# Attention and gated FFN on one core: paired attention bursts, a new order of the first loads, and DMA transposes from unit 7 on

## The chip, the cores and the metric

The kernel runs on one core of a Trainium2 chip. The metric is the device time of one execution in microseconds (us), as the median of several runs. A profile of one execution stands beside it. In it, PE is the matmul engine (TensorE), PEld its weight loads, DVE is VectorE, ACT is ScalarE, POOL is GpSimd, and SP is the engine that issues most of the DMAs.

## The reference, cut to what matters

Attention with a sliding window of 128 and four sink keys, followed by a gated feed-forward layer (FFN), with batch 4, 8 heads, 768 positions, head size 64, and 512 to 1536 to 512 in the FFN:

```python
scores = scale * np.matmul(q, k.transpose(0, 1, 3, 2))
keep = is_sink | in_window            # pos < 4, or 0 <= query - key < 128
a = softmax(np.where(keep, scores, -1e9))
x = (a @ v) with heads side by side   # 3072 x 512
gate = np.maximum(x @ w_gate, 0.0)
val = x @ w_val
out = gate * val @ w_out
```

All arrays are float32 in memory; the kernel computes in bfloat16 with float32 sums.

## The kernel before, in words

**Units.** Attention is cut into 16 units, `U[0]` to `U[15]`: unit i is batch i // 4 and a pair of two heads. For one unit the steps are:

- *Load*: `load_kq("k")`, `load_kq("q")` and `load_v` (three DMAs) bring float32 data into one of four staging tiles `stg`. A unit's five DMAs are issued one after another. `held(x)` (line 328) puts a tiny DVE memset ahead, so that the loads can't start before DVE has got there.
- *Cast*: `casts` turns K, Q and V into bfloat16 (`kn`, `qn`, `vn`), on POOL unless another engine is named.
- *Transpose*: K and Q must have the head dimension on the partitions (`kT`, `qT`). A unit whose flag `xbar` (line 95) is false does it on PE: `T` (line 140), twelve transposes into PSUM and two copies by ACT. A unit whose flag is true does it by two DMAs that SP issues: `X` (line 134). The flag also changes the layout of the K and Q loads: without it each partition reads two runs of 1536 bytes, with it twelve runs of 256 bytes.
- `sinkk` (line 155): two DVE copies from `kT` to `kTs`, which puts the sink keys beside the window keys. They wait for `kT`.
- `S(0)`, `S(1)`, `S(2)` (line 167): scores of a group of key blocks (64x128 matmuls, two heads at once), exp on ACT, and the mask multiply on DVE. In batch 0 the mask is instead added by a bias matmul.
- `norm(u, part)` (line 253), for two halves: `V` (line 187) makes the sums and the weighted values by 128x64 matmuls, and four DVE operations divide and write `xT`.

**Chunks.** The FFN is cut into 96 chunks (`chunk`, line 270), 24 for each batch: one of two halves of 384 positions by one of twelve blocks of 128 hidden columns. A chunk is four matmuls into `gp`, relu on ACT, four matmuls into `vp`, and the DVE multiply into `hT`. `gp` and `vp` take turns in three PSUM buffers (`ps_gv`); S and V of a unit take turns in two (`ps_at`) once the chunks have begun. The second FFN matmul, `ffn2` (line 287), goes three at a time behind each chunk as soon as half a batch is complete; it multiplies with `wo`.

**Order.** The order on every engine is that of the program; nothing reorders it. A list `stages` holds the attention work: a first stage and then six for each unit, made by `unit_stages` (line 360): `s(0)`, `v`, `s(1)`, `t`, `s(2)` and the `norm` of part 0. `v` is the `norm` of part 1 of the unit before. `s(0)` also issues `X` of the next unit. `t` prepares the next unit (`T` or nothing, then `sinkk`), issues one unit's loads and a part of the weights, and casts the unit three further on. `PLAN` (line 414) says how many stages have to be out before chunk ci: the pairs (ci, number of stages) are joined by straight lines, so that one stage falls to about every chunk. When chunk 24 begins, batch 1 is being multiplied while batch 2's attention is on its way.

**Weights.** POOL's queue loads `w_gate` and `w_val` in four column parts (`load_w`), and `w_out` in three row parts (`load_wo`); these loads stand in the order of POOL's casts. `load_wo(0)`, `(1)` and `(2)` are issued in stage `t` of units 5, 6 and 7, ahead of that stage's casts.

**Start.** K of unit 0 is loaded by SP and Q of unit 0 by ACT; V of unit 0 and all other loads follow on SP. POOL builds the identity and the first two bias patterns (`setup_pool`), DVE the rest (`setup_m0`, `setup_m1`). Sixteen matmuls on the identity warm PE.

Of the kernel before, what the change touches and what calls it, by code (L numbers as in the profile page):

```python
# [33 lines left out]
def kernel(  # L34
# [12 lines left out]
    nc = tc.nc  # L47
    B, H, S, D = q.shape
    assert (B, H, S, D) == (4, 8, 768, 64)
    NP = H // 2  # L50
# [21 lines left out]
    kT = [const.tile([128, 872], BF16, name=f"kT{i}") for i in range(2)]  # L72
# [15 lines left out]
    class Unit:  # L88
# [3 lines left out]
        def __init__(self, i):  # L92
            self.i, self.b, self.p, self.s = i, i // NP, i % NP, i % 2
            self.kn, self.qn, self.vn, self.stg = kn[i % 3], qn[i % 3], vn[i % 4], stg[i % 4]
            self.xbar = self.b>1
            self.biased = self.b == 0

        def staging(self, x):
# [24 lines left out]

        def cast(self, what, eng):

            if what in "kq":
                eng.tensor_copy((self.kn if what == "k" else self.qn)[:],  # L127
                                self.staging(what).rearrange("p h (n d) -> p n h d", d=64))
                return
            eng.tensor_copy(self.vn[:, 0:6, :, :], self.staging("v")[:, 0:6, :, :])  # L130
            eng.tensor_copy(self.vn[0:24, 6, :, :], self.staging("v")[0:24, 6, :, :])  # L131
            eng.tensor_copy(self.vn[0:4, 1:6:2, :, :], bc(self.vn[0:4, 0, :, :], 3))  # L132
# [7 lines left out]
        def T(self, first):  # L140

            s = self.s
            if first:
                ps = ps_gv.tile([128, 1024], BF16, name="tk", tag="gv")[:]
                pq = ps_op.tile([128, 1024], BF16, name="tq", tag="op")[:]
            else:
                both = ps_at.tile([128, 2, 1024], BF16, name="tkq", tag="at")
                ps, pq = both[:, 0, :], both[:, 1, :]
            for x, p_ in ((self.kn, ps), (self.qn, pq)):
                for t in range(6):  # L150
                    nc.tensor.transpose(p_[:, t * 128:(t + 1) * 128], x[:, t, :, :].rearrange("p h d -> p (h d)"), ident[:])
            for p_, dst, cp in ((ps, kT[s], nc.scalar.copy), (pq, qT[s], nc.scalar.copy)):
                cp(dst[:, 0:S].rearrange("d (p n) -> d p n", n=6), p_[:, 0:S].rearrange("d (n p) -> d p n", n=6))

        def sinkk(self):

# [50 lines left out]
    def load_w(c):  # L207
        n = d_ff // 4
        for w, dst in ((moe_w_gate, wg), (moe_w_val, wv)):
            nc.gpsimd.dma_start(out=dst[:, :, c * n:(c + 1) * n],  # L210
                                in_=w.rearrange("(ko ki) n -> ki ko n", ki=128)[:, :, c * n:(c + 1) * n])
# [16 lines left out]
    def setup_slot(s):  # L228
        nc.vector.memset(kT[s][:, S:872], 0.0)

    cp, ms = nc.vector.tensor_copy, nc.vector.memset

    def setup_m0():

        ms(bias[0:4, 0:128], 0.0)
        ms(bias[0:4, 128:255], NEG)
        cp(bias[:, 255:503], bias[:, 503:751])
        ms(bias[0:4, 255:503], 0.0)
        ms(bias[0:4, 503:627], NEG)

    def setup_m1():

        band, sk = (lambda a, b: bias[:, 503 + a:503 + b]), (lambda n: bias[:, 255:255 + n])
        cp(bias[:, 754:1002], sk(248))
        cp(bias[:, 1002:1253], band(0, 251))
        cp(bias[:, 1253:1397], sk(144))
        cp(bias[:, 1397:1417], band(0, 20))
        nc.vector.tensor_scalar(out=msk[:], in0=bias[:], scalar1=-1.0, scalar2=None, op0=Alu.is_ge)
# [53 lines left out]
    with tc.manual_schedule():  # L302
        U = [Unit(i) for i in range(B * NP)]
        on_array = []

        def at(x):
            return U[x] if 0 <= x < len(U) else None

        def casts(u, what, eng=nc.gpsimd):
            for w in what:  # L310
                u.cast(w, eng)

        warm_ps = []

        def warm(n):

            if not warm_ps:
                warm_ps.append(ps_at.tile([128, 2, 512], F32, name="warm", tag="at"))
            for _ in range(n):
                nc.tensor.matmul(out=warm_ps[0][:, 0, 0:128], lhsT=ident[:], rhs=ident[:], start=True, stop=True,  # L320
                                 skip_group_check=True)

        def load(x):
            U[x].load_kq("k", nc.sync)
            U[x].load_kq("q", nc.sync)
            U[x].load_v(nc.sync)

        def held(x):

            if x < len(U):  # L330
                nc.vector.memset(U[x].stg[0:1, 0:1], 0.0)
                load(x)

        U[0].load_kq("k", nc.sync)
        U[0].load_kq("q", nc.scalar)
        U[0].load_v(nc.sync)
        for x in range(1, 4):
            load(x)
        nc.vector.memset(ones[:], 1.0)
        setup_pool()  # L340
        nc.scalar.activation(ee[0][:, 0, 0, 0:64], ones[:], Act.Exp, bias=0.0, scale=1.0)
        for x in range(4):
            nc.vector.memset(vn[x][:, 6, :, :], 0.0)
        setup_slot(0)
        setup_slot(1)
        setup_m0()

        warm(16)
        casts(U[0], "k")
        casts(U[0], "q", nc.vector)  # L350
        casts(U[0], "v")
        casts(U[1], "kqv")
        casts(U[2], "kqv")
        load(4)
        setup_m1()


        stages = []

        def unit_stages(x):  # L360
            u, prev, nxt = U[x], at(x - 1), at(x + 1)

            def s(gi):
                def f():
                    if gi == 0 and u.p == 0:
                        xTs[u.b] = xpool.tile([128, NP, S], BF16, name="xT")
                    if gi == 0 and nxt is not None and nxt.xbar:
                        nxt.X()
                    u.S(gi)
                return f  # L370

            def v():
                if prev is not None:
                    norm(prev, 1, ps_at if on_array else ps_gv)

            def t():
                if nxt is not None:
                    if not nxt.xbar:
                        nxt.T(not on_array)
                    nxt.sinkk()  # L380
                if x == 0:
                    load_w(0)
                    load(5)
                elif x == 1:
                    load_w(1)
                elif x == 3:
                    load_w(2)
                    load(6)
                elif x == 4:
                    load_w(3)  # L390
                    load(7)
                elif 5 <= x:
                    held(x + 3)
                    if x < 8:
                        load_wo(x - 5)
                if at(x + 3) is not None:
                    casts(at(x + 3), "kqv")
            return [s(0), v, s(1), t, s(2), lambda: norm(u, 0, ps_at if on_array else ps_gv)]

        def first():  # L400
            U[0].T(True)
            U[0].sinkk()
        stages.append(first)
        for x in range(len(U)):
            stages += unit_stages(x)
        stages.append(lambda: norm(U[-1], 1))

        si = 0
        f2 = deque()
        total = len(stages)  # L410

        ORDER = [(0, h, m) for g in range(0, FM, 3) for h in range(2) for m in range(g, g + 3)]
        ORDER += [(b, h, m) for b in range(1, B) for h in range(2) for m in range(FM)]
        PLAN = ((0, 28), (24, 50), (48, 74), (71, 98))

        def want(ci):
            for (c0, w0), (c1, w1) in zip(PLAN, PLAN[1:]):
                if ci <= c1:
                    return w0 + (w1 - w0) * (ci - c0) // (c1 - c0)
            return total  # L420
        count = {}
        n = S // 2
        for ci, (b, h, m) in enumerate(ORDER):
            if b not in hTs:
                hTs[b] = hpool.tile([128, FM, S], BF16, name="hT", tag="hT")
            while si < min(total, want(ci)):
                stages[si]()
                si += 1
            if not ci:
                on_array.append(1)  # L430
            chunk(b, h * n, n, m)
            for _ in range(min(3, len(f2))):
                f2.popleft()()
            count[b, h] = count.get((b, h), 0) + 1
            if count[b, h] == FM:
                for t in range(3 * h, 3 * h + 3):
                    for mm in range(FM):
                        f2.append(lambda b=b, t=t, mm=mm: ffn2(b, t, mm, tail=b == B - 1))
        while f2:
            f2.popleft()()  # L440
# [33 lines left out]
```

The softmax here doesn't subtract the row's maximum and nothing guards it: scores larger than these inputs give would overflow.

## Time and profile before

| | |
|---|---|
| median of 8 runs | 265.59 us (263.9 to 269.19) |
| the profiled execution, whole | 265.92 us |
| its span, first to last instruction | 264.1 us |
| mean granted PE clock | 0.994 |
| DMA packets | 77318, of them 64496 under 512 bytes |
| wait of DVE for ACT's kT, in all | 7.0 us, 5 times |
| wait of POOL's kn cast for the K loads, in all | 33.7 us, 6 times |

The span is the time between the first and the last instruction of the profiled execution; 1.8 us lie around it. A row of the timeline gives the start, the length, the engine, the line of the code, the operation with the tiles written and read, and how many instructions were merged into the row. In brackets stand the idle time of the engine before it and what ended that. The row of a group of matmuls begins with the first and lasts to the modelled end of the last, so that successive rows overlap. "SPq" is the queue of SP: its rows show how long an issue kept it.

### The profile page before, as it was taken

Reading aid. Unit: us, or ns where it says so; the run is one execution under the profiler, and the core shown is the slowest. Engines: PE = TensorE matmul, PEld = TensorE weight load, DVE = VectorE, ACT = ScalarE, POOL = GpSimd, SP = SyncE. Lnnn points to the kernel's source line nnn. Section 1 sums busy time; section 2 is a strip of 40 time slices with the busy share of each in tenths; the row PEclk is TensorE's granted clock in tenths of the full one; section 3 lists DMA queues with packets and bytes.
Section 4 is the critical chain, followed back from the end, with each engine's and each line's share of the span. In section 5 each row is a group of like instructions: output and inputs, shape, how many; then the busy total and the mean of one; then the engine's idle time right before and its main releaser. Section 6 shows DMA issues by size and latency. Waiting matters only on the chain.

```text
span 264.1 us, 5117 instructions
## 1 busy us (share of the span) xinstructions
PE 250.6 (95%) x1968; PEld 139.4 (53%) x1992; DVE 145.6 (55%) x318; ACT 115.4 (44%) x186; POOL 63.0 (24%) x102
## 2 busy tenths in 40 slices
PE   3999899999978999999999999999999999999994
PEld 3555555665544555555555555555555555555441
DVE  3399969777762566665747566575656232322100
ACT  2777855656423444344344434434433323333211
POOL 5787359524213040221305050000000000000000
PEclk9999999999997999999999999999999999999999
DMA  7999999997989390939469391311011011111132
GB/s 195 313 293 222 245 242 230 222 228 138 177 134 199 93 220 10 236 86 174 109 139 181 83 201 40 63 40 42 0 42 40 2 41 40 40 42 40 40 119 79
DMA packets 77318, 33.54 MB, mean 127 GB/s; under 512 B 64496, under 2 KB 74224, under 8 KB 77296
## 3 DMA queue, kind: packets, MB, share of 16 engines
q1 hardware_dynamic: 71216, 28.12, 47.7%
q0 software_dynamic: 5808, 4.72, 11.4%
q10 hardware_dynamic: 272, 0.39, 0.4%
q8 instruction: 15, 0.25, 0.4%
q14 instruction: 7, 0.06, 0.1%
HBM read 28.51 MB, written 6.29 MB: 132 GB/s over the span
## 4 chain that ended last, share of the span: by engine, by line
PE 69%; DMA 18%; SPq 5%; POOL 3%; issue 3%; ACT 0%; POOLq 0%; ACTq 0%
PE op L294 23%; PE gp L275 20%; PE vp L281 18%; DMA stg<-in_v_dram 11%; PE ops L201 5%; DMA stg<-in_q_dram 5%; PE sps L179 3%; SPq L120 3%; DMA wo<-in_moe_w_out_dram 3%; SPq L112 2%; POOL vn L132 1%; SPq L122 1%; POOL vn L131 1%; POOL vn L130 1%; POOL qn L127 0%
## 5 line engine op out<-in xcount | busy, mean ns | idle before, releaser
L275 PE MATMUL gp<-xT,wg 128*128 128x384 bf16 x384 | 79.3, 330 | 0.0
L281 PE MATMUL vp<-xT,wv 128*128 128x384 bf16 x384 | 78.6, 328 | 0.5 <-DVE R L260 0.4
L278 ACT ACTIVATE gs<-gp 128x384 f32<-128x384 f32 x96 | 47.1, 490 | 72.8 <-PE gp L275 72.1
L283 DVE TENSOR_TENSOR hT<-gs,vp 128x384 bf16<-128x384 f32 x96 | 52.8, 551 | 43.1 <-PE vp L281 40.9
L294 PE MATMUL op<-wo,hT 128*128 128x512 bf16 x264 | 70.9, 380 | 3.8 <-DMA wo<-in_moe_w_out_dram 2.5
L183 ACT ACTIVATE ee<-sps 128x1006 bf16<-128x1006 f32 (+2 forms) x48 | 46.2, 965 | 39.1 <-PE sps L179 39.1
L281 PEld LDWEIGHTS <-wv 128*128 128x128 bf16 x384 | 37.8, 98 | 26.1 <-issue 1.6
L275 PEld LDWEIGHTS <-wg 128*128 128x128 bf16 x384 | 32.9, 98 | 27.5 <-issue 5.3
L294 PEld LDWEIGHTS <-hT 128*128 128x128 bf16 x288 | 28.2, 98 | 26.1 <-issue 0.2
L185 DVE TENSOR_TENSOR ee<-ee,msk 128x1006 bf16<-128x1006 bf16 (+2 forms) x36 | 24.5, 680 | 29.3 <-ACT ee L183 29.3
L127 POOL CAST kn<-stg 128x768 bf16<-128x768 f32 x16 | 13.2, 828 | 60.1 <-DMA stg<-in_k_dram 33.7
L298 ACT COPY ot<-op 128x512 f32<-128x512 f32 x24 | 14.1, 585 | 25.5 <-PE op L294 25.5
L260 DVE STREAM_TRANSPOSE R<-ops 128x384 f32<-128x384 f32 x24 | 13.9, 581 | 12.4 <-PE ops L201 12.2
L130 POOL CAST vn<-stg 128x768 bf16<-128x768 f32 x16 | 13.9, 871 | 23.9 <-DMA stg<-in_v_dram 17.0
L263 DVE STREAM_TRANSPOSE R<-rc 128x384 f32<-128x384 f32 x32 | 18.5, 578 | 1.1
L265 DVE TENSOR_TENSOR xT<-ops,R 128x384 bf16<-128x384 f32 x32 | 17.8, 557 | 1.7
L179 PEld LDWEIGHTS <-kT 64*128 64x128 bf16 x128 | 6.3, 93 | 22.2 <-issue 20.6
L201 PEld LDWEIGHTS <-ones 128*64 128x64 bf16 x288 | 12.3, 109 | 10.3 <-issue 6.9
L201 PE MATMUL ops<-ee,vn 128*64 128x255 bf16 (+8 forms) x288 | 15.5, 233 | 0.4 <-DVE xT L265 0.3
L127 POOL CAST qn<-stg 128x768 bf16<-128x768 f32 x15 | 12.8, 855 | 10.1 <-DMA stg<-in_q_dram 8.3
L179 PE MATMUL sps<-qT,kT 64*128 64x251 bf16 (+2 forms) x128 | 15.1, 257 | 0.1
L179 PE MATMUL sps<-qT,kTs 64*128 64x248 bf16 (+1 forms) x96 | 12.8, 262 | 0.4 <-DVE kTs L160 0.4
(53 smaller groups left out, 130.4 us busy)
## 6 DMA issues: line engine op xcount, KB each, us to landing
stg<-in_k_dram SPq DMA_DIRECT2D x16, 384.0 KB
stg<-in_v_dram SPq DMA_DIRECT2D x32, 192.0 KB
out_dram<-ot SPq DMA_DIRECT2D x24, 256.0 KB
stg<-in_q_dram SPq DMA_DIRECT2D x15, 384.0 KB
wg<-in_moe_w_gate_dram POOLq DMA_DIRECT2D x4, 384.0 KB, 8.2
wv<-in_moe_w_val_dram POOLq DMA_DIRECT2D x4, 384.0 KB, 9.9
wo<-in_moe_w_out_dram POOLq DMA_DIRECT2D x3, 512.0 KB, 7.9
stg<-in_q_dram ACTq DMA_DIRECT2D x1, 384.0 KB
```

What stands on the lines that cost most here:

```text
L127: eng.tensor_copy((self.kn if what == "k" else self.qn)[:], self.staging(what).rearrange("p h (n d) -> p n h d", d=64))
L179: nc.tensor.matmul(out=ps[:, h, c:c + w], lhsT=self.kw(j, r), rhs=qT[s][r, qa:qa + w], start=not self.biased, stop=True, skip_group_check= ...
L183: nc.scalar.activation(x, ps[:, :, 0:c], Act.Exp, bias=0.0, scale=scale)
L185: nc.vector.tensor_tensor(x, x, bc(msk[:, m0:m0 + c], 2), op=Alu.mult)
L201: nc.tensor.matmul(out=ps[1 - what][64 * h:64 * h + 64, qa - q0:qa - q0 + w], lhsT=self.vn[:, j, h, :] if what else ones[:], rhs=ee[s][:, ...
L263: nc.vector.transpose(r[:, 1, 0:w], bass.AP(a.tensor, a.offset, [a.ap[0], [1, nb], [0, 32]]))
L265: nc.vector.tensor_tensor(xTs[u.b][:, u.p, c0:c0 + w], o[:, 0:w], r[:, 1, 0:w], op=Alu.mult)
L275: nc.tensor.matmul(out=gp[:, 0:n], lhsT=wg[:, ko, m * 128:(m + 1) * 128], rhs=x[:, ko, c0:c0 + n], start=ko == 0, stop=ko == KO - 1)
L278: nc.scalar.activation(gs[:, 0:n], gp[:, 0:n], Act.Relu, bias=0.0, scale=1.0)
L281: nc.tensor.matmul(out=vp[:, 0:n], lhsT=wv[:, ko, m * 128:(m + 1) * 128], rhs=x[:, ko, c0:c0 + n], start=ko == 0, stop=ko == KO - 1)
L283: nc.vector.tensor_tensor(hT[:, m, c0:c0 + n], gs[:, 0:n], vp[:, 0:n], op=Alu.mult)
L294: nc.tensor.matmul(out=op, lhsT=hTs[b][:, m, t * 128:(t + 1) * 128], rhs=wo[:, m, :], start=m == 0, stop=m == FM - 1)
```

## The change

- `xbar` becomes true from unit 7 on (it was from unit 8 on): unit 7, the last pair of heads of batch 1, is now loaded in the other layout and transposed by DMA.
- Units 8 to 15 (batches 2 and 3) have three stages instead of six: `v` and `s(0)`, `t` and `s(1)`, and `norm` of part 0 and `s(2)` are each issued together. `PLAN` is adapted: 12 stages fall to 24 chunks there.
- The three loads of `w_out` move from stage `t` of units 5, 6, 7 to that of units 4, 5, 6.
- The first loads are K0, Q0, K1, Q1, V0, V1, all by SP; then units 2 and 3. Unit 0's K is cast by DVE and its Q by ACT; POOL casts K and Q of unit 1 ahead of V of unit 0.
- For unit 0 the copies out of PSUM after the transposes are cut into halves, with K's on DVE and Q's on ACT.
- `setup_m0` runs on POOL, directly after `setup_pool`; `setup_m1` runs after unit 0's `sinkk`.
- In stage `t` of unit 0 the casts of unit 3 stand ahead of `load_w(0)` instead of behind it.

```diff
-            self.xbar = self.b>1
+            self.xbar = i>6
...
+            cp = eng.copy if eng is nc.scalar else eng.tensor_copy
             if what in "kq":
-                eng.tensor_copy((self.kn if what == "k" else self.qn)[:],
-                                self.staging(what).rearrange("p h (n d) -> p n h d", d=64))
+                cp((self.kn if what == "k" else self.qn)[:],
+                   self.staging(what).rearrange("p h (n d) -> p n h d", d=64))
...
-            for p_, dst, cp in ((ps, kT[s], nc.scalar.copy), (pq, qT[s], nc.scalar.copy)):
-                cp(dst[:, 0:S].rearrange("d (p n) -> d p n", n=6), p_[:, 0:S].rearrange("d (n p) -> d p n", n=6))
+            for a, b in ((0, 64), (64, 128)) if self.i == 0 else ((0, 128),):
+                for p_, dst, cp in ((ps, kT[s], nc.vector.tensor_copy if self.i == 0 else nc.scalar.copy), (pq, qT[s], nc.scalar.copy)):
+                    cp(dst[:, 0:S].rearrange("d (p n) -> d p n", n=6)[:, a:b, :],
+                       p_[:, 0:S].rearrange("d (n p) -> d p n", n=6)[:, a:b, :])
...
-    cp, ms = nc.vector.tensor_copy, nc.vector.memset
-
     def setup_m0():
 
+        cp, ms = nc.gpsimd.tensor_copy, nc.gpsimd.memset
...
     def setup_m1():
...
+        cp = nc.vector.tensor_copy
...
-        U[0].load_kq("k", nc.sync)
-        U[0].load_kq("q", nc.scalar)
-        U[0].load_v(nc.sync)
-        for x in range(1, 4):
-            load(x)
+        for x in range(2):
+            U[x].load_kq("k", nc.sync)
+            U[x].load_kq("q", nc.sync)
+        for x in range(2):
+            U[x].load_v(nc.sync)
+        load(2)
+        load(3)
         nc.vector.memset(ones[:], 1.0)
         setup_pool()
+        setup_m0()
...
-        setup_m0()
-
         warm(16)
-        casts(U[0], "k")
-        casts(U[0], "q", nc.vector)
+        casts(U[0], "k", nc.vector)
+        casts(U[0], "q", nc.scalar)
+        casts(U[1], "kq")
         casts(U[0], "v")
-        casts(U[1], "kqv")
+        casts(U[1], "v")
         casts(U[2], "kqv")
         load(4)
-        setup_m1()
...
+                if x == 0:
+                    casts(at(x + 3), "kqv")
                 if x == 0:
                     load_w(0)
                     load(5)
...
                 elif x == 4:
                     load_w(3)
                     load(7)
+                    load_wo(0)
                 elif 5 <= x:
                     held(x + 3)
-                    if x < 8:
-                        load_wo(x - 5)
-                if at(x + 3) is not None:
+                    if x < 7:
+                        load_wo(x - 4)
+                if x and at(x + 3) is not None:
                     casts(at(x + 3), "kqv")
-            return [s(0), v, s(1), t, s(2), lambda: norm(u, 0, ps_at if on_array else ps_gv)]
+            def v0():
+                norm(u, 0, ps_at if on_array else ps_gv)
+
+            def both(f, g):
+                return lambda: (f(), g())
+            if x < NP:
+                return [s(0), v, s(1), t, s(2), v0]
+            return [both(v, s(0)), both(t, s(1)), both(v0, s(2))] if x >= 8 else [s(0), v, s(1), t, s(2), v0]
 
         def first():
             U[0].T(True)
             U[0].sinkk()
+            setup_m1()
...
-        PLAN = ((0, 28), (24, 50), (48, 74), (71, 98))
+        PLAN = ((0, 28), (24, 50), (48, 62), (71, 74))
```

## The prediction

> **What bounds the kernel now.** I read the page first (busy times, the 40 slices), then the chain of waits, then the timeline of the two places where TensorE (PE) stops. From the page:
>
> ```profile
> PE 250.6 (95%) x1968; PEld 139.4 (53%) x1992; DVE 145.6 (55%) x318; ACT 115.4 (44%) x186; POOL 63.0 (24%) x102
> PE   3999899999978999999999999999999999999994
> PEclk9999999999997999999999999999999999999999
> ```
>
> PE is busy in every slice but the first, slice 13 (79 to 86 us) and the last. So a gain must be PE work removed, or one of those holes. The timeline shows the hole:
>
> ```profile
> 73.18 0.74 POOL L214 DMA_DIRECT2D wo<-in_moe_w_out_dram  x1
> 79.97 0.58 PE L294 MATMUL op<-wo,hT 128*128 128x512 bf16 x1 [2.52 <-DMA wo<-in_moe_w_out_dram]
> 81.03 1.46 PE L275 MATMUL gp<-xT,wg 128*128 128x384 bf16 x4
> 82.28 1.34 PE L281 MATMUL vp<-xT,wv 128*128 128x384 bf16 x4
> 85.02 0.82 PE L275 MATMUL gp<-xT,wg 128*128 128x384 bf16 x4
> ```
>
> The last third of w_out is issued at 73.18, behind a value cast on POOL, and lands 6.75 us later (chain of waits). PE stands for 2.52 us. Then four gp matmuls take 1.46 instead of 0.82: the trace's clock events put PE at half speed from 79.92 to 83.34. Half of 3.4 us is another 1.7 us lost. The hole costs about 4.2 us.
>
> A second place is close to becoming a hole. Unit 8 is the first whose K and Q are transposed by DMA:
>
> ```profile
> 61.10 0.37 SPq L109 DMA_DIRECT2D stg<-in_k_dram  x1
> 66.45 0.47 SPq L122 DMA_DIRECT2D stg<-in_v_dram  x1
> 67.12 3.20 SPq L137 DMA_TRANSPOSE kT<-kn  x1
> 72.95 0.66 DVE L159 COPY kTs<-kT 128x372 bf16<-128x372 bf16 x1 [1.51 <-DMA kT<-kn]
> ```
>
> Its transpose stands on SP behind unit 9's five loads, and VectorE (DVE) waits 1.51 us for it; PE had just enough stored work. Last, the steady part:
>
> ```profile
> 132.11 0.81 PE L281 MATMUL vp<-xT,wv 128*128 128x384 bf16 x4
> 132.76 0.81 PE L294 MATMUL op<-wo,hT 128*128 128x512 bf16 x3
> 133.41 0.81 PE L275 MATMUL gp<-xT,wg 128*128 128x384 bf16 x4
> ...
> 137.05 0.81 PE L294 MATMUL op<-wo,hT 128*128 128x512 bf16 x3
> 137.79 0.47 PE L201 MATMUL ops<-ee,ones 128*64 128x255 bf16 x8
> ```
>
> Between groups of full-array matmuls starts lie 0.65 apart (132.11, 132.76, 133.41). From op to the 128x64 matmuls of V it is 0.74. Single records in the trace give the same: whenever the tile form changes (128x128, 64x128, 128x64), about 97 ns pass between the end of one stream and the start of the next.
>
> **What the Trainium skill says.**
> - "TensorEngine Tiling (Array Packing)", Key Properties: changing the tiling mode drains TensorE. The trace agrees: 97 ns at each change.
> - "TensorE: Matmul & The Clock Gate", Part 1: after about one idle window of 3.4 us the array runs at half clock, and the windows run free. The trace agrees on the half clock and the length (3.41 us), but a gap of 2.52 us was enough.
> - Same page, Architectural detail: ScalarE and VectorE are strict FIFO. The 1.51 us wait above held all DVE work behind it.
> - "DMA: Bandwidth & Descriptors", Queues, rings and completion order: an engine goes round its queues packet by packet. The trace agrees roughly: from 22 to 24 us each engine moved 24.6 packets of 256 bytes from SP's queue and 22.9 of 768 bytes from POOL's. So small packets crawl while weights load.
>
> **The change, part by part.** The sum is against the profiled execution: 264.1 us span plus 1.8 around it, 265.92; the median shown is 0.33 lower.
>
> *w_out one step earlier.* Each third moves up one unit. The last then follows unit 8's casts instead of unit 9's; before, that slot issued at 62.47. Landing takes 6.8 to 7.9, so even with 3 us of slip it is there by 74, against a need at 77. Gain 2.5 + 1.7 = 4.2, if nothing else stops PE in the same window.
>
> *Unit 7 by DMA instead of PE.* Removed from PE: two groups of six transposes, at 58.82 to 59.66, 0.84 us; from ACT two copies of 0.8, off the path. Added: two DMA transposes on SP, and unit 7's K and Q loads now in 256-byte pieces (12 per partition instead of 2). Packet records: 256 bytes take about 20 ns, 1536 bytes 78; per engine 192 x 20 = 3.8 us against 32 x 78 = 2.5, so 1.3 us more DMA time in a stretch (42 to 60) where the DMA share is 1.1 to 1.3. What counts is the place: the transposes stand on SP behind unit 8's loads. Before, those landed at 59.8, and unit 8's transpose landed 1.1 us after its last preceding load. So unit 7's kT lands at 60.9 at the earliest; with 1.3 us of added bytes at 62.2; with 256-byte pieces sharing round robin with w3 and the earlier w_out third, 63 to 67. I take 63.2. DVE reaches the copy kTs<-kT of unit 7 at about 60 and stands there; behind it are the hT multiply of the current chunk, the mask and the norm. PE can run one more chunk: three gp/vp buffers, so it stops at the gp that needs this chunk's vp buffer freed. That gp was at 63.45; less 0.84 and 0.2 (start-up) it is 62.4. DVE needs 1.05 from landing to freeing (0.45 kTs, 0.06 memset, 0.55 hT). PE loss = landing + 1.05 - 62.4 = 1.85 at 63.2. A half-clock window costs 1.7 more; with three chances in ten, 0.5. The memset that holds unit 9's loads is behind the same copy: they start 2.6 us later (63.7 against 61.1), unit 8's kT lands near 75.7 instead of 72.9, and DVE waits there again; PE, late itself by then, loses about 1.2. Sum +3.5.
>
> *Bursts in units 8 to 15.* V and S, with a chunk between them before, now follow each other: in each unit two pairs merge, and each merger saves one form change (V to S is itself one; 28.87 to 29.02 is one in the trace, with a wait in it). 2 x 8 x 0.097 = 1.55 us. The DVE queue of a burst is norm (0.58 + 0.23 + 0.58 + 0.56) plus mask 0.69, 2.7 us, within the two chunks (over 4 us) to the next burst; were it not, a chunk's gp would wait up to 0.6, at most 5 us over 8 units. The exp (1.0) delays relu by under 1, covered by the third buffer. I take -1.55 (-2 to +1).
>
> *First loads.* Landings show K0 at 5.06, Q0 at 5.49, V0 at 7.2, then about 1.14 us for each K or Q: one stream at full rate. Q0 on SP instead of ACT does not make it faster; K0 comes earlier (about 4.4), Q0 about 5.2 to 5.5, K1/Q1 at 7.8 instead of 9.4, V0 at 9.5 instead of 7.2. The second transpose group needs Q0's cast (now ACT, about 0.8, before DVE 0.84), so it stays near 6.5. The halved copies on DVE and ACT (0.8 each before) free S from waiting for qT to 8.36, but the bias matmuls hold PE to 8.3 anyway. V0's cast ends near 11.3 against a need at 12.7. The wait of T(1) for qn at 10.4 (0.4) goes. The bias set-up on POOL hides in its idle time before K1 lands; the mask set-up moves behind kTs on DVE and is due at 8.94. Gain 0.2 (0 to 1).
>
> *Casts of unit 3 ahead of the first weights.* On POOL load_w(0) slips from 16.67 to about 20.9 and load_w(1) follows at once. With landings of 8.8 and 10.7 the vp weights come at 30 to 32, against a first vp at 32.07 (which had waited 0.41 for DVE). Cost 0 to 1.5; in return unit 5's Q no longer stops PE at 35.07 (0.31). I take 0.
>
> Sum: -4.2 - 0.84 - 0.2 + 3.5 - 1.55 = -3.3. Span 260.8, own time 262.6, against the median 262.3; forecast 262.4.
>
> **Rivals.** (A) The forecast: faster, with a wait at unit 7's kTs. (B) kT lands by 61.5 and the wait hides: then only -6.8 remains, 258.8. For it: DVE waited 1.51 at unit 8 without loss. Against: unit 8's loads alone ended at 59.8. (C) kT lands near 65.5: 4.15 lost at once, 1.7 of half clock, about 1 at unit 8; the sum is 0 and the time 265.6. (D) Slower: unit 7's 256-byte loads crawl beside w3 and w_out, Q7 holds up everything behind it on SP, and kT lands at 69. PE loses 7.65, the half clock 1.7, the next unit 1.0: 10.35 - 6.8 = +3.5, 269.1. It decides from a landing of about 67.5 on. For it: V5's second half, issued at 23.05 beside two weight loads, kept SP for 4.65 us and landed 12 us after issue. Against: by 59.8 all of U7, U8, w3 and one third of w_out had landed before; the volume grows by 1.3 us plus one third (3 us).
>
> **How the numbers follow.** A 0.45, B 0.18, C 0.17, D 0.20. About 0.5% (1.3 us) is what a measurement of this kernel tells from no change. Faster = A + B = 0.63, within = 0.17, slower = 0.20. Range 258.6 to 267.5: it holds A and C and most of B, takes in the bounds of first weights (+1.5) and bursts (+1), and leaves out D's upper part and B's lower tail. A alone: 260.5 to 264.2.
>
> **What would show it.** Right: no wait of op for wo; DVE kTs<-kT waiting for DMA 2 to 4 us near 60; a PE gap of 1 to 2.5 us there; unit 7's transposes gone from PE; V directly followed by S from about 76 us on, with per-unit time down by 0.2. Wrong: PE waiting at gp on DVE beside the bursts, the first vp waiting on wv by over 1.5 us, PE clock low at another place, or a kT landing outside 61.5 to 65.

## The result, and the profile after

The changed kernel takes 268.97 us (median of 11 runs, 266.62 to 269.76), the kernel before on the same chip 265.53 (median of 32). The ratio is 1.0134, with a 95% interval of 1.0106 to 1.0163: slower by about 3.5 us, where 3.2 us faster was forecast. Runs that the chip disturbed are left out of all ratios; two experiments (e10, e14) kept too few undisturbed runs for one. The profiled execution took 267.88 us, its span is 266.1.

The page's busy times, slices and granted clock of the changed kernel:

```profile
PE 247.9 (93%) x1957; PEld 138.9 (52%) x1980; DVE 146.9 (55%) x315; ACT 114.5 (43%) x185; POOL 62.6 (24%) x106
PE   5997679998699999999999999999999999999993
PEclk9999999999799999999999999999999999999999
```

TensorE has less work (247.9 against 250.6), yet the span is longer. The hole of slices 12 and 13 (7 and 8 tenths before; the prediction named only 13) is gone; in its place stand one in slices 10 and 11 (60 to 73 us) and a shallow one in slices 4 to 6 (20 to 40 us). The low clock has moved along, from slice 13 to slice 11. The timeline of the new hole, all engines:

```profile
67.83 0.30 DVE L162 COPY kTs<-kT 128x372 bf16<-128x372 bf16 x1 [5.34 <-DMA kT<-kn]
...
68.17 0.54 DVE L286 TENSOR_TENSOR hT<-gs,vp 128x384 bf16<-128x384 f32 x1
...
68.76 1.44 PE L278 MATMUL gp<-xT,wg 128*128 128x384 bf16 x4 [3.39 <-DVE hT L286]
...
70.00 1.49 PE L284 MATMUL vp<-xT,wv 128*128 128x384 bf16 x4
...
71.81 0.82 PE L278 MATMUL gp<-xT,wg 128*128 128x384 bf16 x4
```

Read it upwards from the stopped engine. TensorE stood 3.39 us for a buffer that the multiply into hT frees; that multiply stood on DVE behind the copy kTs<-kT of unit 7; DVE had stood there 5.34 us for the transposing DMA, which landed at 67.81. The four gp matmuls after it take 1.44 instead of 0.82: the clock events give half speed from 68.19 to 71.60. SP's queue shows why the DMA was late:

```profile
52.14 0.37 SPq L109 DMA_DIRECT2D stg<-in_k_dram  x1
52.60 3.67 SPq L109 DMA_DIRECT2D stg<-in_q_dram  x1
56.37 5.20 SPq L120 DMA_DIRECT2D stg<-in_v_dram  x2
61.66 1.01 SPq L122 DMA_DIRECT2D stg<-in_v_dram  x1
62.84 2.91 SPq L138 DMA_TRANSPOSE kT<-kn  x1
```

The first four rows are unit 8's loads. The second number is how long an issue kept SP; those of Q and V kept it 3.67 and 5.20, so the transpose, whose input was ready when the cast of K ended at 51.1, was issued 10.7 us after the first of them. The third w_out load no longer stops anything; the row of op in the page's groups has no wait for wo left:

```profile
L278 PE MATMUL gp<-xT,wg 128*128 128x384 bf16 x384 | 79.1, 329 | 4.0 <-DVE hT L286 3.4
...
L284 PE MATMUL vp<-xT,wv 128*128 128x384 bf16 x384 | 78.8, 328 | 1.7 <-DMA wv<-in_moe_w_val_dram 1.7
...
L297 PE MATMUL op<-wo,hT 128*128 128x512 bf16 x265 | 70.6, 379 | 1.2
```

The steady part, TensorE's timeline, shows the bursts as meant, V followed at once by S:

```profile
121.89 0.81 PE L297 MATMUL op<-wo,hT 128*128 128x512 bf16 x3
122.64 0.47 PE L204 MATMUL ops<-ee,ones 128*64 128x255 bf16 x8
122.96 0.45 PE L204 MATMUL ops<-ee,vn 128*64 128x255 bf16 x8
123.35 0.28 PE L182 MATMUL sps<-qT,kT 64*128 64x251 bf16 x2
```

The shallow hole comes from the first group of edits (the order of the first loads, the casts and copies of units 0 and 1, the moved set-ups, and unit 3's casts). TensorE's timeline at 27 us, and POOL's ahead of it:

```profile
27.05 0.51 PE L152 MATMUL tk<-ident,kn 128*128 128x128 bf16 x6 [1.58 <-POOL kn L128]
```

```profile
23.06 0.87 POOL L213 DMA_DIRECT2D wg<-in_moe_w_gate_dram  x1
...
25.40 0.77 POOL L213 DMA_DIRECT2D wv<-in_moe_w_val_dram  x1
26.13 0.86 POOL L128 CAST kn<-stg 128x768 bf16<-128x768 f32 x1
```

With unit 3's casts moved ahead of load_w(0), four weight issues follow each other on POOL, 3.1 us in all, and unit 4's cast waits behind them.

To see where time goes and comes back, here is the start of DVE's multiply into hT for some chunks (us from the span's start, from the records of each profiled execution; e1 and e11 are explained below):

| chunk | before | after | after minus before | e1 | e11 |
|---|---|---|---|---|---|
| 0 | 34.06 | 36.42 | +2.36 | 35.43 | 34.77 |
| 12 | 56.76 | 59.78 | +3.02 | 57.63 | 57.33 |
| 18 | 66.94 | 73.56 | +6.62 | 67.82 | 67.95 |
| 23 | 77.64 | 84.73 | +7.09 | 78.52 | 78.15 |
| 36 | 113.26 | 116.69 | +3.43 | 110.95 | 110.58 |
| 66 | 186.68 | 189.01 | +2.33 | 183.27 | 182.91 |
| end | 264.14 | 266.11 | +1.97 | 259.69 | 259.34 |

In this execution the start loses 3.0 up to chunk 12, unit 7 (chunks 12 to 18) 3.6, w_out gives back 3.7 (23 to 36), and the bursts 1.1 in the five units from chunk 36 to 66, 0.22 for each.

### The profile page after: what moved, and what is told of

The parts are those of the page before. It is cut to its first block, busy times and chain, and to the rows that moved or that the text cites. A ratio compares the mean times of both kernels' runs of the same rounds, so it can differ in the third digit from the quotient of the medians.

```text
span 266.1 us, 5090 instructions
## 1 busy us (share of the span) xinstructions
PE 247.9 (93%) x1957; PEld 138.9 (52%) x1980; DVE 146.9 (55%) x315; ACT 114.5 (43%) x185; POOL 62.6 (24%) x106
## 4 chain that ended last, share of the span: by engine, by line
PE 80%; DMA 15%; issue 1%; ACT 1%; SPq 1%; DVE 0%; POOL 0%; ACTq 0%; POOLq 0%; DVEq 0%
PE gp L278 23%; PE op L297 23%; PE vp L284 22%; PE ops L204 6%; DMA stg<-in_q_dram 6%; DMA wv<-in_moe_w_val_dram 4%; PE sps L182 4%; DMA stg<-in_v_dram 3%; DMA kT<-kn 2%; SPq L112 1%; PE tkq L152 1%; PE sps L177 0%; ACT ee L186 0%; ACT kT L155 0%; ACT qT L155 0%
## 5 line engine op out<-in xcount | busy, mean ns | idle before, releaser
L278 PEld LDWEIGHTS <-wg 128*128 128x128 bf16 x384 | 34.2, 98 | 34.2 <-issue 8.7
L188 DVE TENSOR_TENSOR ee<-ee,msk 128x1006 bf16<-128x1006 bf16 (+2 forms) x36 | 25.6, 711 | 10.2 <-ACT ee L186 10.1
L128 POOL CAST kn<-stg 128x768 bf16<-128x768 f32 x15 | 12.5, 835 | 55.4 <-DMA stg<-in_k_dram 33.6
L131 POOL CAST vn<-stg 128x768 bf16<-128x768 f32 x16 | 13.3, 828 | 24.8 <-DMA stg<-in_v_dram 19.6
L162 DVE COPY kTs<-kT 128x372 bf16<-128x372 bf16 x16 | 6.7, 421 | 17.0 <-DMA kT<-kn 9.1
```

The source lines that it names most:

```text
L128: cp((self.kn if what == "k" else self.qn)[:], self.staging(what).rearrange("p h (n d) -> p n h d", d=64))
L188: nc.vector.tensor_tensor(x, x, bc(msk[:, m0:m0 + c], 2), op=Alu.mult)
L278: nc.tensor.matmul(out=gp[:, 0:n], lhsT=wg[:, ko, m * 128:(m + 1) * 128], rhs=x[:, ko, c0:c0 + n], start=ko == 0, stop=ko == KO - 1)
```

## The experiments

In each diff, "-" is the kernel that the experiment starts from. Ratios are to the kernel before on the same chip.

**e1: the changed kernel with unit 7 transposed by TensorE again.**

```diff
-            self.xbar = i>6
+            self.xbar = i>7
```

> The changed kernel, but unit 7 is transposed by PE again (transposing DMAs from unit 8 on). Theory 1 (unit 7's kT lands late, DVE stands, PE runs dry and its clock halves): the PE stop of 3.4 us near 68 us and the half-clock window after it are gone, 0.8 us of transposes come back; the median falls from 269.0 to about 265 (264 to 266). Theory 2 (the order of unit 3's casts and the first weights is the main cost): it falls by under 2 us. Rival (bursts or first loads cost): no fall beyond 1 us.

262.48 us, ratio 0.9822 [0.9752, 0.9891]. The list of waits has one short wait for a transposing DMA left, at unit 8:

```profile
DVE kTs L162 <- DMA kT<-kn: 1.0, 1, 1.0
```

(total us, times, longest us.) The median falls by about 6.5 us where about 4 was expected; the section on the prediction comes back to the rest. One flag turns the loss into a gain; everything else of the change together is a gain. **e12** is the same kernel again, measured 14 times: 262.45 us, 0.9907 [0.9874, 0.9940].

**e2, e3: unit 3's casts behind load_w(0) again,** in the changed kernel (e2) and together with e1's edit (e3).

```diff
-                if x == 0:
-                    casts(at(x + 3), "kqv")
...
-                if x and at(x + 3) is not None:
+                if at(x + 3) is not None:
```

> The changed kernel, but in stage t of unit 0 the first weights are again ahead of unit 3's casts on POOL. Theory 1: the first chunk comes 2 to 3 us earlier, but unit 7's kT comes when the DMAs let it, so PE only stands longer there; the median stays within 1 us of 269. Theory 2: PE no longer waits 1.6 us for unit 4's kn and 1.65 us for the first wv, and the median falls by 2 to 3.5 us to about 266.

> The changed kernel without either of the two. Theory 1 and 2 together: about 3 us below the first of these runs, 261 to 263, under the kernel before (265.5) by 3 to 4 us, as the gains (w_out earlier, bursts) are all that is left. Rival (bursts or first loads cost): 264 or more.

e2: 268.63 us, 1.010 [0.9988, 1.0213]; e3: 263.99 us, 0.9859 [0.9755, 0.9962]. Chunk 0 does come earlier (32.66 in e2, 33.41 in e3), but the same POOL work then falls on the next unit. TensorE's timeline of e3:

```profile
36.21 0.51 PE L152 MATMUL tkq<-ident,kn 128*128 128x128 bf16 x6 [2.44 <-POOL kn L128]
```

The place of these casts moves a stop; it doesn't remove it. e2 came out within 1 us of the changed kernel, as the first theory has it, and in its trace DVE still waits 4.09 for unit 7's kT. e3 lies between the times that its expectation gave and decides nothing. Neither run shows these casts as the cause of the slower kernel.

**e4, e8, e7: one part alone, put into the kernel before.** e4 has the bursts and their PLAN, e8 the thirds of w_out one unit earlier, e7 unit 7 by DMA:

```diff
-            self.xbar = self.b>1
+            self.xbar = i>6
```

> The kernel before with the bursts of units 8 to 15 and their plan alone. By the form changes saved (16 x 97 ns) 1.6 us less than before, 264.0; the traces of both kernels give 0.22 us less for each unit, 1.8 us. If the bursts cost something where DVE is loaded, 265.5 or more.

> The kernel before with w_out's thirds one unit earlier, alone. If the wait of op for w_out and the half clock behind it cost 4.2 us: the wait is gone and the median is 3 to 4 us below before. If another wait is next (the casts of unit 8 or unit 8's kT, held up by the earlier weights): under 2 us.

> The kernel before with transposing DMAs from unit 7 on, alone. If unit 7 is the whole loss: a PE stop of 2 to 4 us with a half-clock window near 65 us comes in addition; the later stop for w_out shrinks as PE comes later; the median is 2 to 5 us above the kernel before. If it only hurts together with the earlier w_out or the new start: within 1 us of before.

e4: 265.95 us, 0.9935 [0.9893, 0.9976]. e8: 262.03 us, 0.9882 [0.9804, 0.9960]. e7: 270.31 us, 1.0171 [1.0076, 1.0267], and its timelines, of DVE and then of TensorE, show three stops, the last one longer than before, with the clock at half from 82.78 to 89.61:

```profile
63.35 0.32 DVE L159 COPY kTs<-kT 128x372 bf16<-128x372 bf16 x1 [3.63 <-DMA kT<-kn]
```

```profile
64.30 0.81 PE L275 MATMUL gp<-xT,wg 128*128 128x384 bf16 x4 [1.75 <-DVE hT L283]
77.69 0.81 PE L275 MATMUL gp<-xT,wg 128*128 128x384 bf16 x4 [1.23 <-DVE hT L283]
83.52 0.59 PE L294 MATMUL op<-wo,hT 128*128 128x512 bf16 x1 [3.94 <-DMA wo<-in_moe_w_out_dram]
```

Two parts gain and one loses, and the signs stand apart clearly. e7's time is as expected, its course is not. Alone, unit 7's kT landed at 63.33 (the completion records), and TensorE stopped for 1.75 at unit 7 and 1.23 at unit 8: close to the prediction's 63.2, 1.85 and 1.2. But the stop for w_out didn't shrink, it grew from 2.52 to 3.94, since the last third went out at 76.75 instead of 73.18, and two half-clock windows followed instead of one. 1.75 + 1.23 + 1.42 + 1.7 - 0.84 = 5.3, against 5.1 between the two spans. The delay was passed on down the program.

**e6: unit 7's loads in pieces of 256 bytes, but its transposes on TensorE.** Is it the layout of the loads or the transposing DMA?

```diff
-            self.xbar = i>6
+            self.xbar = i>7
+            self.tiled = i>6
...
-            if self.xbar:
+            if self.tiled:
                 eng.dma_start(...)
...
```

(T then copies the PSUM tile without its rearrangement, since the pieces already lie in order.)

> The changed kernel with unit 7's loads in pieces of 256 bytes as there, but transposed by PE (the copies out of PSUM are then plain). If the place of the transposes on SP is the cause: no PE stop near 68, within 1 us of the run that undoes unit 7 (262.5). If the small pieces are the cause: the casts of unit 7 and the loads of unit 8 come late, PE stops by 2 us or more between 58 and 80 us, and the median is 265 or more.

262.93 us, 0.9916 [0.9885, 0.9948], that of e12. The profiled execution, at 265.27 well above the median, did stop for 2.34 at 77.77, which the expectation had as a sign for the small pieces; there it was unit 8's transpose, issued beside the last third of w_out, that took 8.54 us to land. In the median the small pieces alone cost nothing that can be told. What remains is the transposing DMA and what it waits behind.

**e5: unit 7's two transposes ahead of unit 8's loads on SP.** The changed kernel; unit 8's loads, the second third of w_out and unit 8's casts go behind unit 7's X in s(0) of unit 6.

```diff
                     if gi == 0 and nxt is not None and nxt.xbar:
                         nxt.X()
+                    if gi == 0 and x == 6:
+                        held(8)
+                        load_wo(1)
+                        casts(at(8), "kqv")
...
```

> The changed kernel with unit 7 still transposed by DMA, but its two transposes stand on SP ahead of unit 8's loads (unit 8's loads, casts and the second third of w_out move from stage t of unit 5 to the s(0) of unit 6). If the place on SP is the cause: kT of unit 7 lands by about 56 instead of 67.8, DVE waits under 1 us for it, PE doesn't stop near 68, and the median is about 262 to 263. If the 256-byte pieces or the transposes themselves are the cause: a wait of DVE for kT near 60 us stays and the median is 266 or more.

A clear miss: 272.46 us, 1.0246 [1.0131, 1.0360], slower still. The transpose was issued 9.6 us earlier and landed only 1.9 us earlier. Two rows of the chain of waits (start, length; unit 7's transpose, then unit 8's):

```profile
53.28 12.69 DMA kT<-kn
...
75.87 7.99 DMA kT<-kn
```

and POOL's timeline just before:

```profile
50.16 0.74 POOL L213 DMA_DIRECT2D wg<-in_moe_w_gate_dram  x1
50.89 0.75 POOL L213 DMA_DIRECT2D wv<-in_moe_w_val_dram  x1
51.62 0.76 POOL L217 DMA_DIRECT2D wo<-in_moe_w_out_dram  x1
```

A fourth weight load followed at 55.43. The DMA itself took 12.69 us. For the units of batch 3, when no weights are loaded, the same DMA takes 2.73 to 3.35 in the same kernel. Unit 8, shifted back, was then late too and stopped TensorE for 4.16 at 84.76. This brought the next question: is it the place on SP, or the weights in flight?

**e9 and e13: the weights moved away, with either order on SP.** e9 is e5, e13 the changed kernel, both with load_w(3) one unit earlier and the thirds of w_out one unit later, the first behind its stage's casts. (The expectations have e5's landing as 64.53, when 15 of the DMA's 16 parts were in; the last came at 65.96.)

```diff
                     load_w(2)
+                    load_w(3)
                     load(6)
                 elif x == 4:
-                    load_w(3)
                     load(7)
-                    load_wo(0)
...
```

> e5_x7_first (unit 7's two transposing DMAs ahead of unit 8's loads on SP) with the weight loads of POOL taken away from around them: the last quarter of w_gate and w_val goes out one unit earlier, right behind the third quarter, and the thirds of w_out one unit later, as in the kernel before. In e5 kT of unit 7 was issued at 53.28 and landed at 64.53, 11.25 us later, with four weight loads of POOL in flight. Theory 1 (the transposes starve beside POOL's weight loads): kT lands within 5 us of its issue, so by about 59, the DVE no longer waits for it, and the TensorE's stop for gp behind hT near 67 (2.03 in e5) and its half clock window are gone; the w_out wait of the kernel before (about 2.5, and a half clock window) is back, so the time is 264 to 267. Theory 2 (the transposes themselves or the small pieces of unit 7's own loads are slow, whatever else runs): kT still lands at 63 or later and the time stays at 268 or above. Theory 3 (the casts of unit 7 are late, which the moved weights make earlier): issue moves ahead of 53 and the delay from issue to landing stays near 11.

> The changed kernel with its own order on SP (unit 7's transposing DMAs behind unit 8's loads), but with POOL's weight loads taken away from around them as in e9: last quarter of w_gate and w_val one unit earlier, thirds of w_out one unit later. Known so far: transposes late on SP, weights in flight: kT of unit 7 lands at 67.8 (the changed kernel); early on SP, weights in flight: 64.5 (e5); early on SP, no weights: 57.0 (e9). Theory 1 (the weight loads alone make it late, since they also hold up unit 8's loads ahead of the transposes on SP): kT of unit 7 is issued by 59 and lands by about 62, the DVE waits for it 1 at most, no TensorE stop for gp near 68, and the time is that of e9, 264 to 267. Theory 2 (either alone is enough: behind unit 8's loads it is late even with the weights away): issue after 61, landing after 65, a TensorE stop for gp of over 1, and 267 or more.

e9: 265.38 us, 1.0006 [0.9964, 1.0048]. e13: 270.78 us, 1.0181 [1.0101, 1.0261]. e9's transpose on SP's queue, with no weight load issued beside it (e5's stands above, at 53.28):

```profile
52.84 1.32 SPq L138 DMA_TRANSPOSE kT<-kn  x1
```

The four corners, from the completion records and the timelines:

| kernel | unit 7's transposes on SP | POOL's weight loads | kT(7) issued, landed | DVE waited | TensorE's stop at unit 7 / at unit 8 |
|---|---|---|---|---|---|
| after | behind unit 8's loads | beside | 62.84, 67.81 | 5.34 | 3.39 / none |
| e5 | ahead | beside | 53.28, 65.96 | 4.04 | 2.03 / 4.16 |
| e13 | behind | moved away | 59.51, 62.73 | 0.76 | none / 3.52 |
| e9 | ahead | moved away | 52.84, 57.04 | none | none / none |

With the weights away, kT lands 3.2 to 4.2 us after its issue and nothing stops at unit 7, in either order: the first theory holds for the landing. For the time it holds in e9 alone. In e13 the loss moved on. POOL's and DVE's rows, from the timelines of e13:

```profile
63.33 1.49 POOL L217 DMA_DIRECT2D wo<-in_moe_w_out_dram  x2
74.87 0.82 POOL L128 CAST kn<-stg 128x768 bf16<-128x768 f32 x1 [10.04 <-DMA stg<-in_k_dram]
```

```profile
62.75 0.31 DVE L162 COPY kTs<-kT 128x372 bf16<-128x372 bf16 x1 [0.76 <-DMA kT<-kn]
...
78.66 0.29 DVE L162 COPY kTs<-kT 128x372 bf16<-128x372 bf16 x1 [6.29 <-DMA kT<-kn]
```

The two thirds of w_out went out at 63.33, together with unit 9's loads; those crawled (K of unit 9 took 10.96 us to land), unit 8's transpose stood behind them on SP until 75.47, and TensorE stopped for 3.52 at 80.08, then for 2.37 at 86.02, for the last third of w_out; four half-clock windows lie there on end (78.60 to 92.25). The first stop is the same collision, one unit later; the second is a price of the later w_out. In e9 unit 8's transpose, beside three w_out loads, took 9.89 us from issue to landing; DVE waited 4.57 for it, TensorE just got by without a stop at unit 8, and lost 1.84 in three short waits for w_out.

**e10, e14: the first group alone, in the kernel before** (first loads, split copies, moved setup, casts of units 0 and 1; e14 has unit 3's casts moved as well).

> The kernel before with the reordered first loads, the split first copies and the moved setup and casts of units 0 and 1 alone; without the casts of unit 3 ahead of the first weights, the earlier w_out, the bursts and unit 7 by DMA. The record's own term for this group was -0.2. If it is only a start: the first scores begin about 0.9 us earlier (as in the changed kernel, 7.48 against 8.40) and chunk 0 comes earlier by up to 1.5, but the w_out wait of the kernel before later takes it back in part: ratio 0.992 to 1.001. If the group is a loss by itself: above 1.002.

> The kernel before with the first group of edits whole: reordered first loads, split first copies, moved setup, casts of units 0 and 1, and unit 3's casts ahead of the first weight loads; w_out, bursts and unit 7 as before. e10 had this without unit 3's casts and gave no ratio (264.41 to 271.5). The record said -0.2 for the first loads and 0 (to +1.5) for the casts. e12 against e11, which differ in this group alone, was +1.56 (262.45 to 260.89). If the group costs what that difference says: ratio 1.004 to 1.008. If the w_out wait of the kernel before, which comes later, swallows it (the group's delay lets w_out land in time): 0.997 to 1.002. If it gains: below 0.997.

e10: 270.64 us (264.41 to 271.5), e14: 267.88 us (263.4 to 270.0), no ratio for either. Inconclusive: neither a gain nor a loss is shown.

**e11: the two gains without the rest,** that is e4 and e8 together in the kernel before.

> The kernel before with the two parts that were measured as gains alone: w_out one unit earlier (-3.8 in e8) and the bursts (-1.7 in e4). If they add up: -5.3, ratio 0.980 (0.977 to 0.984). If the bursts' gain is another when w_out is no longer waited for: nearer to e8 alone, 0.986 to 0.989.

260.89 us, 0.9849 [0.9786, 0.9912]: the lowest median of all, below both kernels. The ratio lies between the two ranges that were expected, and its interval reaches into both. Its page:

```profile
PE 247.7 (96%) x1969; PEld 140.4 (54%) x1992; DVE 147.7 (57%) x318; ACT 115.5 (45%) x186; POOL 61.1 (24%) x102
PE   3999899999999999999999999999999999999993
PEclk9999999999999999999999999999999999999999
```

No hole is left after the start, and the clock stays whole. e12, which has the first group in addition, read 1.56 us more on the same chip (expectation: equal, or up to 1% above); the two intervals overlap, so a cost of the first group is likely but not shown. The traces point the same way: e12's TensorE waits 1.31 for unit 4's kn at 27.00, and e11's doesn't wait there; and DVE's multiply of chunk 12 starts at 57.6 to 59.8 in six traces with the whole group (the changed kernel, e1, e5, e9, e12, e13), at 56.5 to 57.3 in four with the old start (the kernel before, e7, e8, e11).

## Why the prediction was wrong

The mechanism was foreseen, its size wasn't. The step that failed is the term for unit 7, with kT landing at 63.2, PE losing 1.85, the half clock 0.5 and unit 8 1.2, in sum +3.5: in the changed kernel kT landed at 67.81, and the term, less the 0.84 of transposes, was worth 6 to 8 us instead of 2.7. A smaller part is the first group, put at -0.2 and 0 and worth about +1.6 (likely, not shown). Of the signs of being wrong that the prediction named, three came: the first vp waited 1.65 on wv, the clock was low at another place, and kT landed outside 61.5 to 65.

- **Landing.** It was put together from unit 8's old landing, 1.3 us of added bytes and about a microsecond for sharing with the weights. Measured: 67.81, above the point of 67.5 from which the slower rival was to decide. The sharing was the term that was mis-sized: e13, with the same order on SP but no weights beside it, lands at 62.73, near the 62.2 that the prediction had before it added any sharing, so the weight loads are worth 5.1 us. e7 shows where the 63.2 would have held: with the old start and w_out at its old place. Rival D named the place and the mechanism (loads that crawl beside w3 and w_out, and Q and V that hold SP), and its time, 269.1, is 0.1 from the median. So close is luck: it had the landing at 69, a loss at unit 8 that didn't come, and a small gain at the start instead of a loss. One of its premises is not borne out: by e6 the pieces of 256 bytes are not what costs.
- **Stop.** The formula (landing + 1.05 - 62.4) gives 6.46 for the landing at 67.81. TensorE came to the closed buffer at 65.4 instead, 3.0 later, as late as chunk 12 was, and lost 3.39 there. Lateness and stop together make the 6.4 of the formula. How far the late start itself delayed the landing isn't shown.
- **Half clock.** Put at three chances in ten. It came in the profiled execution, and more than once in others: one window lowers the mean clock of an execution by 0.0064 (half of 3.41 over 266). Ten of the changed kernel's twelve recorded executions have 0.976 to 0.987, as much as two to four windows; the eighteen of e1 and e12 have 0.992 to 1.0. Where in those executions the windows lie isn't known; in the traces of e9 and e12 one covers about the last 2 us of the span.
- **Unit 8.** DVE waited 2.75 there, but TensorE didn't stop: 0 instead of 1.2.
- **Unit 7 in sum.** In the trace 3.39 + 1.7 - 0.84 = 4.3 where +2.7 net was forecast; e1 and e12 against the changed kernel's ratio say 2.3% to 3.2%, 6 to 8 us. The further windows are a part of that: between the mean clocks of the changed kernel, 0.9854, and of e12, 0.9957, lie about 2.7 us (an estimate, the difference times 266), where the trace's one window is 1.7.
- **w_out.** Forecast -4.2; e8 gave -3.8 in the medians, -3.1 by the ratio (1 to 5 us by its interval), and the wait is gone. Right within that; the forecast took the half clock as certain, while 4 of the 24 executions of the kernel before that stand beside e8 have a mean clock of 1.0.
- **Bursts.** Forecast -1.55; e4 gave -1.7 by the ratio (0.6 to 2.8), the trace 0.22 per unit. Right. The norm and mask of a burst never held up a chunk in the steady part.
- **First loads.** The first scores start at 7.48 instead of 8.40, within the range given; but K and Q of unit 1 landed at 8.37 and 9.59, no earlier than before (8.26 and 9.40), where 7.8 was forecast. **Unit 3's casts** were put at 0 because only the landing of the first weights was looked at; that did cost (1.65 at the first vp). What was overlooked are the issues themselves: four in a row keep POOL for 3.1 us, unit 4's casts stand behind them, and TensorE lost 1.58 and then 0.94 there. e2 shows that behind load_w(0) the casts had no free place either.

Summed from the runs by their ratios: -3.1 (w_out) and -1.7 (bursts), +1.6 for the first group (likely, not shown) and +6 to +8 at unit 7 make +2.8 to +4.8; measured was +3.5.

Two statements of the Trainium skill bear on the explanation. "DMA: Bandwidth & Descriptors", Queues, rings and completion order, says that a DMA engine goes round the queues that have work, a packet at a time. The trace of e5 agrees for a part of the 12.69 us: from 58 to 63 us 676 packet records of 256 bytes from SP's queue stand beside 642 of 1024 from POOL's, about one for one, so that the small packets get a fifth of the bytes. It differs for another part: from the transpose's issue at 53.28 to 57.3 SP's queue moved no data packet at all, while POOL's moved 892. Why SP's queue stood still is not shown. "TensorE: Matmul & The Clock Gate", Architectural detail, has VectorE as a strict FIFO; the trace agrees, since the multiply into hT, whose inputs were there by 64.7, ran only behind the copy at 67.83.

What stays open: what the first group costs by itself, and whether a spacing of the weights exists that clears both unit 7 and unit 8. It wasn't tried beyond e9, which reads 3 us more than e12 (unit 7 transposed by TensorE, w_out early) on the same chip; another queue than SP's for the transposes wasn't tried either.

## What to carry to other kernels

Before work is taken from a busy engine and given to a DMA, look at what else is in flight at that hour and at what stands ahead of it in the issuing queue: 0.84 us of TensorE's time was bought with a DMA that took between 2.7 and 12.7 us, with a strictly ordered engine waiting on it. If a transfer is late, try its order and its competition apart from each other; here moving it forward with the weights still beside it made things worse. And count the issues of loads as work of the engine that issues them: here four in a row kept POOL for 3.1 us ahead of unit 4's cast.

## What the runs showed of the hardware that was not expected

- The same transposing DMA (128x768, bf16, within the on-chip memory) took 2.73 us from issue to landing with little beside it, 4.96 in the changed kernel's unit 7, 7.99 and 9.89 beside w_out loads, and 12.69 beside four weight loads.
- In all the kept traces together, the 15 transposing DMAs of K that were issued while a weight load was in flight took 4.2 to 12.7 us (median 6.4; the 4.2 is unit 7 in e9, beside the last 0.7 us of a load), and each landed only after the weight loads issued before it had landed; the 119 others took 2.7 to 5.4 (median 3.3).
- Short stops were followed by the half clock: 2.52 us in the kernel before, 2.03 in e5 (window 67.25 to 70.66), and even 1.45 in e9 and 1.31 in e13, where TensorE waits for unit 4's K (windows from 28.34 and 27.40). 1.58 at the same place in the changed kernel and 2.34 in e6 led to none. So these runs give no length of a stop that decides; what does is not shown.
